# Attention, four experts and a gated MLP on one core: the experts' tail as a ranked list, W2's loads first on GpSimd's queue, GELU without GpSimd, w_out's last row in thirds

## The chip, the cores and the metric

The kernel runs on one core of one Trainium2 chip. A core has TensorE (PE, matmuls), VectorE (DVE), ScalarE (ACT), GpSimd (POOL) and SyncE (SP, which here only issues DMAs). Each engine works its own instruction stream in order and waits on semaphores for the others. The metric is the device time of one execution in microseconds; lower is better.

## The reference

Three layers in a row, in float32, for 4 batches of 448 positions. The inputs are random; cut to what is computed:

```python
# 1: attention, 12 heads of 64, scores capped
scores = cap * np.tanh(scale * (q @ k.T) / cap)
x = softmax(scores) @ v                       # 4 x 448 x 768
# 2: four experts, of which each position takes two
logits = x @ w_gate
topk = np.argpartition(-logits, 2, axis=-1)[..., :2]
w = softmax over the two chosen logits
for e in range(4):
    a = softmax(causal(scale * (x @ wq[e]) @ (x @ wk[e]).T))
    out += chosen(e) * w[e] * (a @ (x @ wv[e]) @ wo[e])
# 3: MLP with spatial gating
h = gelu(x @ w_in)                            # tanh form, 0.044715
u, v = halves of h (512 columns each)
v_s = w_sg @ (layernorm(v) * g_ln) + b_sg     # over positions
return x + (u * v_s) @ w_out
```

## The kernel before

**Numbers.** Where more than single precision's fast form is needed, a matrix is held as two rounded parts, hi and lo (names in _h and _l, type fp32r), and a product is three matmuls; transposes, the experts' scores and the attention run in plain fp32. `rnd` makes the hi part on a chosen engine ("v" VectorE, "a" ScalarE, "p" GpSimd), `rest` the lo part. The weight w_out comes in double precision, and `w_out(k, i, ...)` turns one half of a row k (384 columns) into hi and lo: a load, bit operations on VectorE (tiles `wum`), three operations on GpSimd (tiles `wuw`), and two stores to DRAM (`wud`), from which `wu_h` and `wu_l` are loaded later.

**Stages.** Attention runs in 25 slots, one pair of heads each: six slots make a batch. In the first slots the product W2 = wo w_in is made besides and stored (`w2d`). The experts of a batch follow its attention by some slots; what of them goes into which slot stands in `PLAN`: `queries_keys` (18 matmuls each, tile qk), `values_chunk` (18 matmuls, tile v; its last four columns are the gate's logits, copied to lg), `weigh` (scores `a` of a chunk of 112 positions, a mask operation with the row's maximum on VectorE, exp on ScalarE into `pe`), `gates`, `settle` (reciprocals on VectorE, then eight scalings of pe on GpSimd), `turn` (transposes `tr` of pe, evicted to `pt`), `attend` (16 matmuls av, evicted to y). A batch's attention output is finished by `sums` (matmuls with onehot), `invert` (a copy, an addition, a RECIPROCAL of 128x448 on VectorE, a store rd), broadcast loads `rb` by `load_rb`, the multiplication os by rb in `over_sums`, and the split into xh and xl in `in_parts`; `normed` says in which slot.

**Order.** Up to slot 24 all instructions of TensorE, VectorE, ScalarE and GpSimd are held in program order. Behind it stands the tail: the experts of the last two batches and the whole MLP. There the framework's scheduler chooses, by a timeline of its own and by priorities, which follow the order of the code and `tc.high_priority`. `experts_end` gives the tail's experts slot by slot from the same `PLAN`; `together` weaves them with the parts of the MLP. `mlp_a(b)` makes v (hv, four chunks of six matmuls; GELU, normalization, split into vh and vl), `mlp_b(b)` makes u (hu) and the gate products (sp), `mlp_c(b)` the six output rows (o). `mlp_weights(0)` issues the loads of W2 (`w2_h`, `w2_l`) on GpSimd's queue, and `more_weights` loads wo, and wu_h and wu_l when all eight halves of w_out are done (`wu_done`). The halves 29 to 31 of `W_OUT` fall into the tail. `gelu2` takes its scratch from the six buffers of tag tmp. Matmuls appear at L119, transposes at L461 and all other recorded operations at L104, whichever function issues them.

Of the kernel before, what the change touches and what calls it, by code (L numbers as in the profile page):

```python
# [33 lines left out]
LAG, RATIO, LRATIO, AHEAD, EQ, ORD, L1, EL, WC, NCST, D0, D1, D2, PB, XE, SE, START, WARM, Q2, CK, PE, CP_, AD, WR, KD, PTA, PTE, XHA, LGA, SL, GL, YL, GA, GB = 0.4, .9, .35, 150, 1, 3, 1, 1, 500, 1, 3, 3, 2, 1, 1, 0, 500, 12, 1, 2, 0, 0, 0, 6, 0, 4, 2, 4, 4, 0, 0, 0, 1, 0  # L34
GC = float(np.float32(np.sqrt(2.0 / np.pi)))


def drain(gen):
# [34 lines left out]
def build(ctx: ExitStack, tc: tile.TileContext, a: dict):  # L73
# [179 lines left out]
    def slot(i, side):  # L253

        if i == 0:
            ld[0] = load_pair(*pairs[0])
            ld[1] = load_pair(*pairs[1])
        if i + 2 < len(pairs):  # L260
            qk = [at.tile([128, S], F32, tag=t, name=f"{t}{i + 2}", bufs=3) for t in ("qp", "kp")]
            b, hp = pairs[i + 2]
            nc.sync.dma_start(qk[1], a["kT"][b, :, hp, :])
            nc.sync.dma_start(qk[0], a["qT"][b, :, hp, :])
            ld[i + 2] = qk
        if i < len(pairs):
            first = scores(*pairs[i], 0, *ld[i][:2])
            drain(islice(first, 2))
            side("a")
            drain(first)  # L270
        else:
            side("a")
        side("w")
        if i:
            b, hp = pairs[i - 1]
            drain(values(b, hp, ld.pop(i - 1)[2]))
        if 0 < i < len(pairs) - 1:
            b, hp = pairs[i + 1]
            vv = at.tile([CP, 2, NC, D], F32, tag="vv", name=f"vv{b}_{hp}", bufs=3)
            nc.sync.dma_start(vv, a["v"][b, :, 2 * hp:2 * hp + 2])  # L280
            ld[i + 1] = (*ld[i + 1], vv)
        side("a")
        if i < len(pairs):
            drain(scores(*pairs[i], 1, *ld[i][:2]))
        side("p")
        if i:
            b, hp = pairs[i - 1]
            if hp % 2 == 1:
                drain(sums(b, hp // 2))
        if i < len(pairs):  # L290
            add_up(*pairs[i])
        side("n")
# [16 lines left out]
    def in_parts(b, h2):  # L309

        if h2 == 0:
            X[b] = (xp.tile([128, KC, S], F32R, tag="xh", name=f"xh{b}"),
                    xp.tile([128, KC, S], F32R, tag="xl", name=f"xl{b}"))
        (xh, xl), x, o = X[b], os_t.pop((b, h2)), slice(2 * h2, 2 * h2 + 2)
        rnd("v", xh[:, o, :], x)
        rest("v", xl[:, o, :], x, xh[:, o, :])

    def normed(n, place):

        b = (n - 1) // HP - 1  # L320
        step = (n % HP, place)
        if n > B * HP + 4 or b < 0:
# [20 lines left out]
    wu_done = []  # L343

    def w_out(k, i, pool, *tags):

        o = slice(i * DM // 2, (i + 1) * DM // 2)
        w = pool.tile([128, DM], F32R, tag=tags[0], name=f"wuw{k}_{i}")
        me = pool.tile([128, DM], I32, tag=tags[1], name=f"wum{k}_{i}")
        hi, lo = w[:, :DM // 2], w[:, DM // 2:]  # L350
        nc.sync.dma_start(w.bitcast(I64), a["w_out"][:, k, o])
        yield WC
        p, e = from64(w, me[:, :DM // 2], me[:, DM // 2:])
# [5 lines left out]
        wu_done.append((k, i))  # L359
        yield 1.0  # L360

    def queries_keys(b, ep, t):
        xh, xl = X[b]
# [56 lines left out]
        dve.reciprocal(gs, gs)  # L420
        dve.tensor_tensor(wt, wt, gs.unsqueeze(2).to_broadcast([CP, NC, E]), op=ALU.mult)

    def weigh(b, ep, i):

        qk = QKT[b, ep]
        if i == 0:
            for el in range(2):
                CSS[b, ep, el] = sm.tile([CP, NC], F32, tag=f"cs{el}", name=f"cs{b}_{ep}_{el}")
        n = (i + 1) * CP
        qi = slice(i * CP, (i + 1) * CP)  # L430
        gs = [ps_g.tile([128, 512], F32, tag="g", name=f"a{b}_{ep}_{el}_{i}") for el in range(2)]
        for el in range(2):
            r = slice(64 * el, 64 * el + 64)
            mm(gs[el][:CP, :n], qk[r, 0, qi], qk[r, 1, :n], start=True, stop=True)
        for el, g in enumerate(gs):

            m = sm.tile([CP, 1], F32, tag="m", name=f"m{b}_{ep}_{el}_{i}", bufs=4)
            dve.tensor_tensor_reduce(g[:CP, :n], g[:CP, :n], neg[:, S - n:], -1.0, BIG, ALU.add, ALU.min, m)
            pe = PES[b, ep, el, i] = mo.tile([CP, n], F32, tag=f"pe{i}", name=f"pe{b}_{ep}_{el}_{i}", bufs=4)
            act.activation(pe, g[:CP, :n], AF.Exp, bias=m, scale=-1.0, accum_out=CSS[b, ep, el][:, i:i + 1])  # L440
        yield 1.667 * n + 20.0

    def settle(b, ep):

# [48 lines left out]
    def planned(n):  # L493

        work = {"a": [], "s": [], "w": [], "p": [], "t": [], "n": []}
        for b in reversed(range(B)):
            for place, f, *args in PLAN.get(n - (b + 1) * HP - 4, []):
                work[place].append((b, f, args))
        return work

# [8 lines left out]
    def experts_weights(n, place):  # L509
# [13 lines left out]
        if place == "w" and n in parts:  # L523
# [7 lines left out]
    ws = {n: w_out(*divmod(u, 2), *W_OUT[n][1:]) for u, n in enumerate(W_OUT)}  # L531

    def beside(n):

# [21 lines left out]
                    next(ws[n + 1])  # L556
        return side

    def experts_end(n):

        for m in range(n, B * HP + 20):
            work = planned(m)
            for place in "asw":
                yield from run(work[place])
            for place in ("w", "a1"):
                normed(m, place)
            yield from together(run(work["p"]), run(work["t"]), 0.3)
            yield from run(work["n"])
            normed(m, "n")
            if m in W_OUT:  # L570
                yield from ws[m]


    def prepare_weights(pool):
# [79 lines left out]
        slot(n, beside(n))  # L654
    ah.close()
    pe_pin[0] = False
    ex = experts_end(B * HP + 1)

# [22 lines left out]
    def mlp_weights(part):  # L681
        if part == 1:
            yield from more_weights()
            return
        for k in range(2):
# [11 lines left out]
        yield 1.0  # L697

    def more_weights():
        for k in range(2):  # L700
            for i in range(2):
                o = slice(i * DM // 2, (i + 1) * DM // 2)
                t = tmp(f"wo{k}_{i}")[:, :DM // 2]
                nc.sync.dma_start(t, a["wo"][:, k, o])
                rnd("pav"[int(GB) % 10], wo_h[:, k, o], t)
                rest("pv"[int(GB) // 10], wo_l[:, k, o], t, wo_h[:, k, o])
        while len(wu_done) < 8:
            yield 500.0
        for w, d in ((wu_h, wu_d[0]), (wu_l, wu_d[1])):
            for k in range(0, 4, 2):  # L710
                nc.gpsimd.dma_start(w[:, k:k + 2, :], d[:, k:k + 2, :])
        yield 1.0

    def gelu2(out, h, p, n, nm):

        s = tmp(f"gs{nm}")[:p, :n]
        act.activation(s, h, AF.Square)
        pool_e.tensor_scalar(s, s, 0.044715, 1.0, op0=ALU.mult, op1=ALU.add)
        dve.tensor_tensor(s, s, h, op=ALU.mult)
        act.activation(s, s, AF.Tanh, scale=GC)  # L720
        dve.scalar_tensor_tensor(out, s, 1.0, h, op0=ALU.add, op1=ALU.mult)

# [115 lines left out]
        drain(together(mlp_c(2), mlp_b(3), 13440 / C))  # L838
        drain(mlp_c(3))
    elif ORD == 3:  # L840
        drain(together(ex, mlp(((mlp_a, 0), (mlp_b, 0), (mlp_weights, 1), (mlp_a, 1), (mlp_c, 0), (mlp_b, 1), (mlp_a, 2))), LRATIO))
# [69 lines left out]
```

## Time and profile before

| | before |
|---|---|
| median of 3 runs | 559.38 us (558.11 to 561.81) |
| profiled execution | 559.72 us, of which the span on the core is 558.0 |
| TensorE busy | 532.7 us, 95% |
| VectorE busy | 361.4 us, 65% |
| ScalarE busy | 325.7 us, 58% |
| GpSimd busy | 141.4 us, 25% |
| chain that ended last | PE 73%, DVE 16%, ACT 6%, DMA 2% |

The shares are means over the span. Attention fills the first 283 us or so and the tail the rest; VectorE and ScalarE are nearly idle in the last 80 us, and nearly full in parts of the stretch from 290 to 350. The page gives TensorE's clock in tenths of full speed: full speed is 2.4 GHz, and the lower level is 1.2.

### The profile page before, as it was taken

How to read it: one execution, taken by the hardware profiler on the slowest of the kernel's cores; microseconds unless marked ns; L12 is line 12 of the kernel's file. 1: busy time of each engine (PE TensorE's matmuls, PEld its weight loads, DVE VectorE, ACT ScalarE, POOL GpSimd, SP SyncE). 2: the span in 40 equal slices, each digit the busy share in tenths (PEclk: the TensorE clock that was granted, in tenths of full speed). 3: DMA queues.
4: the chain of work that ended last, by engine and by line, in shares of the span. 5: the costliest groups of instructions: out<-in, count | busy, mean ns of one | idle time of the engine just before them, and what ended most of it. 6: DMA issues, size and time to landing. Idle time of an engine off the chain costs nothing.

```text
span 558.0 us, 7562 instructions
## 1 busy us (share of the span) xinstructions
PE 532.7 (95%) x2732; PEld 346.3 (62%) x2732; DVE 361.4 (65%) x725; ACT 325.7 (58%) x508; POOL 141.4 (25%) x180
## 2 busy tenths in 40 slices
PE   7999999899999989999988989999999989999997
PEld 2333333455555554656557655878768879889996
DVE  3899999984666636567567599676631786485300
ACT  5988888688687896577822345353534344253211
POOL 0000122141155251243340364515521131031000
PEclk9999999999999999999999978999999999999999
DMA  8974615752424141322056221010421000000111
GB/s 246 338 217 123 207 51 160 223 175 80 130 67 142 50 140 49 103 71 67 22 158 165 54 59 58 29 58 0 162 101 64 2 0 34 33 34 33 51 49 66
DMA packets 30596, 53.97 MB, mean 97 GB/s; under 512 B 3872, under 2 KB 22880, under 8 KB 30560
## 3 DMA queue, kind: packets, MB, share of 16 engines
q1 hardware_dynamic: 29408, 48.26, 28.2%
q0 software_dynamic: 1152, 5.24, 2.8%
q8 instruction: 21, 0.34, 0.3%
q14 instruction: 15, 0.12, 0.1%
HBM read 41.83 MB, written 11.67 MB: 96 GB/s over the span
## 4 chain that ended last, share of the span: by engine, by line
PE 73%; DVE 16%; ACT 6%; DMA 2%; issue 2%; POOL 1%; DVEq 0%; POOLq 0%; ACTq 0%; SPq 0%
PE o L119 15%; PE po L119 10%; PE s L119 10%; PE qk L119 8%; PE sp L119 7%; PE v L119 5%; ACT p L104 4%; PE a L119 3%; PE hv L119 3%; PE hu L119 3%; PE w2ps L119 2%; PE tr L461 2%; PE av L119 2%; DVE pb L104 2%; DVE rs L104 2%
## 5 line engine op out<-in xcount | busy, mean ns | idle before, releaser
L104 ACT ACTIVATE p<-s,tsc 112x896 f32<-112x896 f32 x96 | 91.4, 1005 | 24.4 <-PE s L119 24.4
L119 PE MATMUL s<-qp,kp 64*112 64x448 f32 x384 | 84.4, 557 | 3.4 <-ACT p L104 3.4
L104 ACT ACTIVATE p<-p,capt 112x1792 f32<-112x1792 f32 x48 | 85.9, 1790 | 1.3
L104 POOL TENSOR_TENSOR pb<-p 112x896 f32<-112x896 f32 x18 | 38.9, 2163 | 166.6 <-ACT p L104 96.9
L119 PE MATMUL po<-p,vv 112*64 112x448 f32 x384 | 77.3, 545 | 0.0
L104 DVE TENSOR_TENSOR pb<-pb,p 112x896 f32<-112x896 f32 x48 | 57.3, 1194 | 16.0 <-ACT p L104 12.3
L119 PEld LDWEIGHTS s<-qp,kp 64*112 64x112 f32 x384 | 30.8, 172 | 50.6 <-issue 21.3
L119 PEld LDWEIGHTS po<-p,vv 112*64 112x64 f32 x384 | 25.5, 136 | 45.0 <-issue 44.0
L104 ACT ACTIVATE pe<-a,m 112x112 f32<-112x112 f32 (+3 forms) x64 | 31.2, 491 | 25.3 <-DVE m L104 24.5
L104 POOL TENSOR_SCALAR pe<-pe,cs 112x112 f32<-112x112 f32 (+1 forms) x64 | 31.6, 519 | 50.3 <-DVE cs L104 50.2
L104 DVE CUSTOM_DVE_ANT_0 a<-a,neg 112x112 f32<-112x112 f32 (+3 forms) x64 | 27.7, 464 | 20.0 <-PE a L119 20.0
L119 PE MATMUL qk<-xh,wqk_h 128*128 128x448 f32 x96 | 38.2, 398 | 2.6 <-DVE xh L104 2.6
L119 PE MATMUL o<-gh,wu_h 128*128 128x448 f32 x96 | 35.6, 371 | 0.8 <-DMA wu_h<-wud 0.8
L119 PE MATMUL o<-gl,wu_h 128*128 128x448 f32 x96 | 35.6, 371 | 0.0
L119 PE MATMUL qk<-xh,wqk_l 128*128 128x448 f32 x96 | 35.4, 369 | 0.0
L119 PE MATMUL a<-qk 64*112 64x112 f32 (+3 forms) x128 | 29.9, 440 | 5.6 <-ACT pe L104 3.4
L119 PE MATMUL o<-gh,wu_l 128*128 128x448 f32 x96 | 35.0, 370 | 0.0
L104 ACT ACTIVATE ob<-o 128x448 f32<-128x448 f32 x24 | 13.0, 541 | 31.5 <-PE o L119 31.3
L119 PE MATMUL v<-wvg_h,xh 128*112 128x260 f32 x96 | 28.7, 299 | 0.7 <-ACT pe L104 0.7
L461 PE MATMUL tr<-ident,pe 112*112 112x112 f32 x160 | 23.7, 261 | 4.9 <-DVE lg L104 1.8
L119 PE MATMUL v<-wvg_h,xl 128*112 128x260 f32 x96 | 27.1, 283 | 0.0
L119 PE MATMUL v<-wvg_l,xh 128*112 128x260 f32 x96 | 27.1, 282 | 0.0
(226 smaller groups left out, 1096.5 us busy)
## 6 DMA issues: line engine op xcount, KB each, us to landing
kp<-in_kT_dram SPq DMA_DIRECT2D x24, 224.0 KB, 3.1
qp<-in_qT_dram SPq DMA_DIRECT2D x24, 224.0 KB, 3.2
vv<-in_v_dram SPq DMA_DIRECT2D x24, 224.0 KB, 3.1
rb<-rd SPq DMA_DIRECT2D x24, 224.0 KB, 4.7
out_dram<-ob SPq DMA_DIRECT2D x24, 224.0 KB, 1.9
wuw<-in_w_out_dram SPq DMA_DIRECT2D x8, 384.0 KB, 3.5
wud<-wuw SPq DMA_DIRECT2D x16, 192.0 KB, 1.9
ws<-in_wqk_dram SPq DMA_DIRECT2D x4, 384.0 KB, 6.0
```

The lines of the kernel that those rows point to most:

```text
L104: ins = f(*args, **kw)
L119: pin(nc.tensor.matmul(*args, **kw))
L461: pin(nc.tensor.transpose(g[:CP, j * CP:(j + 1) * CP], pe[:, j * CP:(j + 1) * CP], ident))
```

## The change

Seven things change, all of them around the tail.

- `experts_end` no longer reads `PLAN`: the tail's experts are one list, `steps()`, and each step is given out at a high priority, ahead of all of the MLP.
- In slot 24 `sums` and `invert` of the last batch come ahead of the experts' work of that slot instead of behind it.
- `weigh` may take two chunks, whose scores share a PSUM bank.
- W2's loads have the highest priority on their queue (12000 instead of 4000).
- `gelu2` does without GpSimd: the square is scaled by the root of 0.044715 on ScalarE, and VectorE adds 1 and multiplies in one operation.
- The first half of w_out's row 2 stays in slot 23; its second half now falls into slot 24, and row 3 is done in three parts of 256 columns within the MLP's list, in tiles of tag tmp (two to a part). `more_weights` waits for the last projections (`projected`) instead of `wu_done`.
- `PTA` goes from 4 to 3, so that the evictions of turn (1,1) go from VectorE to ScalarE, and the last batch's xh is rounded on ScalarE instead of VectorE.

```diff
-LAG, ... KD, PTA, PTE, ... = ..., 0, 4, 2, ...
+LAG, ... KD, PTA, PTE, ... = ..., 0, 3, 2, ...
+GQ = float(np.float32(np.sqrt(0.044715)))
...
+        if i == len(pairs):
+            drain(sums(B - 1, HP // 2 - 1))
+            invert(B - 1)
         side("p")
-        if i:
+        if 0 < i < len(pairs):
...
-        rnd("v", xh[:, o, :], x)
+        rnd("a" if b == B - 1 else "v", xh[:, o, :], x)
...
-    def weigh(b, ep, i):
+    def weigh(b, ep, *chunks):
...
     W_OUT = {11: ("w", xp, "rb0", "rb1"), 14: ("n", at, "ws", "ws"), 17: ("w", at, "ws", "ws"),
-             20: ("n", at, "ws", "ws"), 23: ("w", at, "ws", "ws"),
-             29: ("n", xp, "rb0", "rb1"), 30: ("n", xp, "rb0", "rb1"), 31: ("n", xp, "rb0", "rb1")}
+             20: ("n", at, "ws", "ws"), 23: ("w", at, "ws", "ws"), 24: ("n", at, "ws", "ws")}
...
+        def steps():
+            yield from weigh(b, 0, 2)
+            yield from turn(b - 1, 1, 1)
+            yield from values_chunk(b, 2)
+            yield from weigh(b, 0, 3)
+            yield from values_chunk(b, 3)
+            gates(b)
+            settle(b, 0)
+            yield from queries_keys(b, 1, 0)
+            yield from attend(b - 1, 1)
+            yield from queries_keys(b, 1, 1)
+            yield from turn(b, 0, 0)
+            over_sums(l, 0)
+            over_sums(l, 1)
+            load_rb(l, 2)
+            yield from weigh(b, 1, 0, 1)
...
+        todo = steps()
+        while True:
+            with tc.high_priority(4000):
+                cost = next(todo, None)
...
+        if part == 2:
+            for i in range(3):
+                yield from w_out(3, i, 3, *[lambda dt, name: ml.tile([128, 512], dt, tag="tmp", name=name, bufs=6)] * 2)
+            return
         for k in range(2):
-            with tc.high_priority(4000):
+            with tc.high_priority(12000):
                 nc.gpsimd.dma_start(w2_h[:, k, :], w2_d[0][:, k, :])
...
     def more_weights():
+        while not projected:
+            yield 500.0
...
-        act.activation(s, h, AF.Square)
-        pool_e.tensor_scalar(s, s, 0.044715, 1.0, op0=ALU.mult, op1=ALU.add)
-        dve.tensor_tensor(s, s, h, op=ALU.mult)
+        act.activation(s, h, AF.Square, scale=GQ)
+        dve.scalar_tensor_tensor(s, s, 1.0, h, op0=ALU.add, op1=ALU.mult)
...
-        drain(together(ex, mlp(((mlp_a, 0), (mlp_b, 0), (mlp_weights, 1), (mlp_a, 1), ...
+        drain(together(ex, mlp(((mlp_a, 0), (mlp_weights, 2), (mlp_b, 0), (mlp_weights, 1), (mlp_a, 1), ...
```

How the instructions stand shows three places best. The first is VectorE at the end of slot 24. In the kernel before, the last batch's sums (rs) and the first split of the MLP's y (yh, yl) come there among the masks (ISA) of batch 2:

```order
L104 TENSOR_TENSOR rs_2017<-rs_2017,sum_2_2432 128x448
L104 CAST yh_2503<-y_1431 128x896
L104 ISA a_0_0_2_2491,m_0_0_2_2495<-a_0_0_2_2491,neg 112x336
L104 ISA m_0_0_2_2495 112x1
L104 RECIPROCAL rs_2017<-rs_2017 128x448
L104 TENSOR_TENSOR yl_2504<-y_1431,yh_2503 128x896
L104 ISA a_0_1_2_2492,m_0_1_2_2499<-a_0_1_2_2492,neg 112x336
```

In the changed kernel rs and its RECIPROCAL come just ahead of these rows, which hold the copies lg of batch 2's values chunks 1 and 2, the bit operations (wum) of w_out's half (2,1) and two of the three multiplications os by rb:

```order
L105 COPY lg_2388<-v_1_2410 112x4
L105 TENSOR_SCALAR wum_1_2320<-wuw_1_2319 128x384
L105 ISA a_0_1_2_2515,m_0_1_2_2522<-a_0_1_2_2515,neg 112x336
L105 ISA m_0_1_2_2522 112x1
L105 TENSOR_SCALAR wum_1_2320<-wum_1_2320 128x384 x2
L105 TENSOR_TENSOR os_0_1790<-os_0_1790,rb_0_2381 128x896
L105 SCALAR_TENSOR_TENSOR wum_1_2320<-wuw_1_2319,wum_1_2320 128x384
L105 TENSOR_TENSOR os_2_2062<-os_2_2062,rb_1_2384 128x896
L105 TENSOR_SCALAR wum_1_2320<-wum_1_2320 128x384
L105 SCALAR_TENSOR_TENSOR wum_1_2320<-wuw_1_2319,wum_1_2320 128x384
L105 COPY lg_2388<-v_2_2558 112x4
```

The reciprocal moved ahead of two masks, and os, which stood behind all masks of this pair, moved ahead of the copy lg of chunk 2.

The second place is GpSimd's queue behind the settling of batch 1's second pair (pe). In the kernel before:

```order
L104 TENSOR_SCALAR pe_1_1_3_2285<-pe_1_1_3_2285,cs_1_1_2127 112x448
L687 DMA w_h<-w2d_81 128x1024 x2
L688 DMA w_l<-w2d_82 128x1024 x2
L104 TENSOR_SCALAR gsv_0_2567<-gsv_0_2567 112x512
L104 TENSOR_SCALAR gsv_1_2659<-gsv_1_2659 112x512
```

In the changed kernel:

```order
L105 TENSOR_SCALAR pe_1_1_3_2285<-pe_1_1_3_2285,cs_1_1_2127 112x448
L105 TENSOR_SCALAR wuw_1_2319<-wum_1_2320 128x384
L105 TENSOR_TENSOR wum_1_2320<-wum_1_2320,wuw_1_2319 128x384
L105 TENSOR_TENSOR wuw_1_2319<-wum_1_2320 128x384
L751 DMA w_h<-w2d_81 128x1024 x2
L752 DMA w_l<-w2d_82 128x1024 x2
L105 TENSOR_SCALAR pe_0_0_0_2330<-pe_0_0_0_2330,cs_0_0_2322 112x112
```

W2's loads moved behind the three operations on w_out's half (2,1), which is held in program order, and GELU's operations (gsv) are gone.

The third place is TensorE at the gate products (sp) of batch 2 and output row 1 (o) of batch 1. In the kernel before, the products of the second chunk of positions and then the output row:

```order
L119 MATMUL sp_0_4068<-sg_h,vh_3924 128x448
L119 MATMUL sp_0_4068<-sg_l,vh_3924 128x448
L119 MATMUL sp_0_4068<-sg_h,vl_3925 128x448
L119 MATMUL o_1_4092<-yh_3422,wo_h 128x448
L119 MATMUL o_1_4092<-yl_3423,wo_h 128x448
L119 MATMUL o_1_4092<-yh_3422,wo_l 128x448
```

In the changed kernel, from the last product of the first chunk on:

```order
L120 MATMUL sp_0_4054<-sg_h,vl_3917 128x448
L120 MATMUL o_1_4078<-yh_3525,wo_h 128x448
L120 MATMUL o_1_4078<-yl_3526,wo_h 128x448
L120 MATMUL o_1_4078<-yh_3525,wo_l 128x448
L120 MATMUL sp_0_4054<-sg_h,vh_3916 128x448
L120 MATMUL sp_0_4054<-sg_l,vh_3916 128x448
```

Three of the output row's matmuls moved between the two chunks, and the second chunk's product with vl moved behind the other fifteen.

## Rows read from the trace of the kernel before

**Rows 1.** The page: TensorE's share; its granted clock in 40 slices, in tenths.

```profile
PE 532.7 (95%) x2732; PEld 346.3 (62%) x2732; DVE 361.4 (65%) x725; ACT 325.7 (58%) x508; POOL 141.4 (25%) x180
...
PEclk9999999999999999999999978999999999999999
```

**Rows 2.** What TensorE waited for from 285 us: total, times, longest.

```profile
PE a L119 <- ACT pe L104: 3.4, 3, 2.2
PE a L119 <- ACT qk L104: 1.3, 1, 1.3
PE tr L461 <- ACT pt L104: 0.9, 2, 0.4
PE o L119 <- DMA wu_h<-wud: 0.8, 1, 0.8
...
PE tr L461 <- POOL pe L104: 0.7, 1, 0.7
```

**Rows 3.** Busy time by stage: engines, then PEclk, DMA share, GB/s.

```profile
290.00:300.00 10.00, 7.82 (x45) 4.60 (x38) 8.37 (x20) 2.94 (x9) 1.07 (x2) 1.00 0.60 192
...
340.00:350.00 10.00, 8.73 (x23) 5.42 (x22) 9.33 (x29) 6.83 (x16) 2.82 (x5) 0.66 0.14 41
...
450.00:460.00 10.00, 8.53 (x38) 6.97 (x37) 9.38 (x21) 4.56 (x8) 3.46 (x6) 0.97 0.00 0
460.00:470.00 10.00, 10.00 (x44) 9.14 (x44) 7.83 (x15) 5.26 (x10) 1.69 (x3) 0.86 0.06 23
```

**Rows 4.** VectorE's timeline from 287 us: start, duration, operation, [idle before].

```profile
292.06 2.94 DVE L104 RECIPROCAL rs<-rs 128x448 f32<-128x448 f32 x1
...
302.40 1.09 DVE L104 TENSOR_TENSOR os<-os,rb 128x896 f32<-128x896 f32 x1 [2.06 <-DMA rb<-rd]
...
304.26 1.10 DVE L104 TENSOR_TENSOR os<-os,rb 128x896 f32<-128x896 f32 x1 [0.18 <-DMA rb<-rd]
```

**Rows 5.** TensorE's timeline, 309 to 329 us.

```profile
309.17 2.10 PE L119 MATMUL av<-pt,vp 112*64 112x448 f32 x14
311.20 0.47 PE L119 MATMUL qk<-xh,wqk_h 128*128 128x448 f32 x1
311.51 0.36 PE L119 MATMUL qk<-xh,wqk_l 128*128 128x448 f32 x1
...
328.91 4.00 PE L119 MATMUL av<-pt,vp 112*64 112x448 f32 x16
```

**Rows 6.** GpSimd's timeline at 286 us.

```profile
286.05 1.29 POOL L687 DMA_DIRECT2D w_h<-w2d  x2
```

**Rows 7.** Instructions on the tile wuw: ns min/median/max, first and last start.

```profile
L104 POOL TENSOR_SCALAR wuw<-wum x8: 508/524/1279, 120.7 to 352.4; 128x384 fp32r<-128x384 f32 x8
L104 POOL TENSOR_TENSOR wum<-wum,wuw x8: 1004/1020/1727, 121.3 to 354.7; 128x384 f32<-128x384 f32 x8
...
DMA to landing us min/median/max: 1.8/1.9/4.4
```

**Rows 8.** DMA issues from 280 to 420 us: KB each, us to landing.

```profile
wu_l<-wud POOLq DMA_DIRECT2D x2, 768.0 KB, 9.1
...
w_h<-w2d POOLq DMA_DIRECT2D x2, 512.0 KB, 4.7
```

**Rows 9.** Timelines of TensorE and of VectorE, 455 to 500 us.

```profile
457.14 0.48 PE L119 MATMUL sp<-sg_h,vh 112*128 112x448 f32 x1 [0.72 <-ACT vh L104]
...
458.33 0.47 PE L119 MATMUL sp<-sg_h,vl 112*128 112x448 f32 x1 [0.51 <-DVE vl L104]
...
455.48 0.95 DVE L104 TENSOR_SCALAR vg<-vg,mv,rstd 112x512 f32<-112x512 f32 x1
...
499.77 0.55 DVE L104 TENSOR_SCALAR vg<-vg,mv,rstd 112x512 f32<-112x512 f32 x1
```

**Rows 10.** VectorE's timeline at the gates of the last batch.

```profile
384.93 1.10 DVE L104 TENSOR_TENSOR gt<-gt,eq 112x64 f32<-112x64 f32 x1
```

**Rows 11.** Instructions on the tile gsv (GELU of v).

```profile
L104 POOL TENSOR_SCALAR gsv<-gsv x16: 619/622/1102, 304.7 to 496.2; 112x512 f32<-112x512 f32 x16
```

More of the change, by code (lines that the diff above doesn't have):

```diff
@@ L341, in normed, with w_out @@
             in_parts(b, 2)
[L343 to L350, printed above, removed]
+    projected = []
+    def w_out(k, i, of, w, me):
+        n = DM // of
+        o = slice(i * n, (i + 1) * n)
+        w, me = w(F32R, f"wuw{k}_{i}")[:, :2 * n], me(I32, f"wum{k}_{i}")[:, :2 * n]
+        hi, lo = w[:, :n], w[:, n:]
         nc.sync.dma_start(w.bitcast(I64), a["w_out"][:, k, o])
         yield WC
-        p, e = from64(w, me[:, :DM // 2], me[:, DM // 2:])
+        p, e = from64(w, me[:, :n], me[:, n:])
         rnd("p", hi, p)
@@ L358, in w_out, with scratch @@
             nc.sync.dma_start(wu_d[t][:, k, o], (hi, lo)[t].bitcast(F32))
-        wu_done.append((k, i))
         yield 1.0
+    def scratch(pool, *tags):
+        return [lambda dt, name, tag=tag: pool.tile([128, DM], dt, tag=tag, name=name) for tag in tags]
     def queries_keys(b, ep, t):
@@ L421, in gates @@
         dve.tensor_tensor(wt, wt, gs.unsqueeze(2).to_broadcast([CP, NC, E]), op=ALU.mult)
[L423 removed]
+    def weigh(b, ep, *chunks):
         qk = QKT[b, ep]
[L426 removed]
+        if 0 in chunks:
             for el in range(2):
                 CSS[b, ep, el] = sm.tile([CP, NC], F32, tag=f"cs{el}", name=f"cs{b}_{ep}_{el}")
[L429 to L435, printed above, removed]
+        gs = [ps_g.tile([128, 512], F32, tag="g", name=f"a{b}_{ep}_{el}_{chunks[0]}") for el in range(2)]
+        parts, o = [], 0
+        for i in chunks:
+            n = (i + 1) * CP
+            for el, g in enumerate(gs):
+                r = slice(64 * el, 64 * el + 64)
+                mm(g[:CP, o:o + n], qk[r, 0, i * CP:n], qk[r, 1, :n], start=True, stop=True)
+                parts.append((i, el, n, g[:CP, o:o + n]))
+            o += n
+        for i, el, n, g in parts:
             m = sm.tile([CP, 1], F32, tag="m", name=f"m{b}_{ep}_{el}_{i}", bufs=4)
[L438 removed]
+            dve.tensor_tensor_reduce(g, g, neg[:, S - n:], -1.0, BIG, ALU.add, ALU.min, m)
             pe = PES[b, ep, el, i] = mo.tile([CP, n], F32, tag=f"pe{i}", name=f"pe{b}_{ep}_{el}_{i}", bufs=4)
[L440 to L441 removed]
+            act.activation(pe, g, AF.Exp, bias=m, scale=-1.0, accum_out=CSS[b, ep, el][:, i:i + 1])
+        yield 1.667 * o + 20.0
     def settle(b, ep):
@@ L496, in planned @@
         for b in reversed(range(B)):
-            for place, f, *args in PLAN.get(n - (b + 1) * HP - 4, []):
+            step = n - (b + 1) * HP - 4
+            for place, f, *args in PLAN.get(step, []):
                 work[place].append((b, f, args))
@@ L557, in beside, with experts_end @@
         return side
[L559 to L571, printed above, removed]
+    def experts_end():
+        b, l = B - 2, B - 1
+        def steps():
[14 more added lines that the diff above has]
+            yield from weigh(b, 1, 0, 1)
+            yield from turn(b, 0, 1)
+            in_parts(l, 0)
+            yield from weigh(b, 1, 2)
+            yield from attend(b, 0)
+            in_parts(l, 1)
+            yield from weigh(b, 1, 3)
+            settle(b, 1)
+            over_sums(l, 2)
+            in_parts(l, 2)
+            yield from queries_keys(l, 0, 0)
+            yield from turn(b, 1, 0)
+            yield from queries_keys(l, 0, 1)
+            yield from weigh(l, 0, 0, 1)
+            yield from turn(b, 1, 1)
+            yield from values_chunk(l, 0)
+            yield from weigh(l, 0, 2)
+            yield from attend(b, 1)
+            yield from values_chunk(l, 1)
+            yield from weigh(l, 0, 3)
+            yield from values_chunk(l, 2)
+            yield from values_chunk(l, 3)
+            gates(l)
+            settle(l, 0)
+            yield from queries_keys(l, 1, 0)
+            yield from queries_keys(l, 1, 1)
+            projected.append(l)
+            yield from weigh(l, 1, 0, 1)
+            yield from turn(l, 0, 0)
+            yield from weigh(l, 1, 2)
+            yield from turn(l, 0, 1)
+            yield from weigh(l, 1, 3)
+            yield from attend(l, 0)
+            settle(l, 1)
+            yield from turn(l, 1, 0)
+            yield from turn(l, 1, 1)
+            yield from attend(l, 1)
+        todo = steps()
+        while True:
+            with tc.high_priority(4000):
+                cost = next(todo, None)
+            if cost is None:
+                return
+            yield cost
```

13 lines of the change are left out of this document (6 added, 7 removed).

## The prediction

> **What bounds the kernel now.** I read the engines' shares first: TensorE is busy 532.7 of 558.0 us, and its granted clock dips in the 24th and 25th of 40 slices, 321 to 349 us [rows 1]. So matmul work sets the time, and the change, which removes no matmul, can win or lose only in TensorE's idle time and in the time at the lower clock. Up to about 283.5 us (the last slots of attention) both programs stand alike, instruction for instruction, so I read what follows: TensorE's own waits from 285 us on [rows 2], the granted clock by stage [rows 3], then the stages that hold the losses. The waits add up to some 11 us, in pieces of 0.3 to 2.2. A mean clock of 0.66 over ten microseconds (340 to 350) means that 3.4 of them were lost at 1.2 GHz, behind an idle 1.27 us for a qk eviction [rows 2, 3]. Earlier the clock fell after an idle 2.23 us: the 16 av matmuls there took 4.00 us, where 14 took 2.10 at 2.4 GHz [rows 5]; that is 1.6 lost, and with the rows around it I put it at 2.3. A third dip, around 460 us, costs 0.3 and 1.4 in two windows, 1.7 [rows 3]. After 283.5 us the kernel thus loses about 7.4 us to the clock and 11 to idling. **I price each fall of the clock at 3.4 us**, by the one window that holds a whole one.
>
> The sum is made against the profiled execution's own 559.72 us (span 558.0); the median of the runs is 559.38, 0.06% less.
>
> **The change part by part.**
>
> *Sums and inversion of the last batch ahead of the experts' work.* In the kernel before, the RECIPROCAL of 2.94 us stands at 292.06, ahead of yl and of masks that TensorE waits for [rows 4]. TensorE is busy 7.82 of the ten us from 290 [rows 3]; the 2.18 that lack are three waits behind that RECIPROCAL (a for pe, hu for yl, v for pe), and they go. After the change the sums' matmuls stand where the values of batch 2 begin, at 283.5; with the same 1.0 us until VectorE adds them, 0.6 for that and 2.94, the reciprocal is done at about 288.05 instead of 295.0. The first two os multiplies start 7.4 and 9.3 us behind its end [rows 4], because the broadcast loads are awaited; so they would start at 295.45 and 297.3, and the second one is done at 298.4. But both now stand, with bit operations of w_out's half between them, ahead of the copy lg out of values chunk 2 (the order of VectorE, above), and TensorE's chunk 3 needs that copy. Counting matmuls from 283.5 at the durations of the trace, TensorE comes to chunk 3 at 297.4 and may start it at 299.5: **2.15 us of new idling**. The evictions of turn (1,1), all eight on ScalarE now, I put at 1.25 us between 287 and 297: at least nothing, at most three of some 0.6 each. Net +1.2.
>
> *W2's loads.* They were issued from 286.05 on [rows 6]. Now they stand behind the three GpSimd operations of w_out's half (2,1) (the order of GpSimd, above), 0.52, 1.02 and 1.02 us [rows 7], which wait for the bit operations behind the second os: issue near 302. Landing takes 4.7 us by the row of w_h and 9.1 by the slowest row of that queue [rows 8]: 307 to 311. The first hv now stands behind both key projections, at about 311, so I take nothing, since qk and av hide it; with 9.1, and w_l behind w_h, it is up to 3 us.
>
> *From 311 to 348.* Gone are the waits tr for pe 0.68, tr for pt 0.44, a for pe 2.23 and a for qk 1.27 [rows 2], 4.6 us, and the dips of 2.3 and 3.4: 10.3. In their place: VectorE was about full there, 9.33 of 10 us from 340 on [rows 3], and keeps its work, since the new GELU has two VectorE operations as the old one had. It sheds only the rounding of xh, three operations of about 1 us, which go to ScalarE (6.83 of 10 [rows 3]). So I expect late masks and evictions again: 0.3 and 0.4 early on, and for vh and vl of the first batch between 0.7 (the wait for vh at 457 [rows 9]) and 2.2 (the longest wait of before [rows 2]); I take 1.5, the middle. The thirds are new there. Their six tiles come from the pool that GELU draws on, and GpSimd works them off behind the eight settling operations: two thirds of 2.56 us [rows 7] is 1.7, three of them 5.1, and then a store of 1.9 us [rows 7]. The last tile comes free 7 us after the settling, when the fourth hu wants one: 1.6 us by counting on, bounds 0 and 1.6. That is 3.8 us of new idling, in pieces like those behind which the clock fell; I take **one fall, 3.4**. Net 3.8 + 3.4 - 10.3 = -3.1.
>
> *wu's loads* no longer wait for the last halves' stores but for the projections; between the last qk and their first use there are now some 7.9 us of other matmuls, where before there were 4.3. The 0.8 us for wu_h [rows 2] goes: -0.8.
>
> *Around the last gates.* Beside GpSimd's rounding of wo a small gate operation of 112x64 takes 1.10 us [rows 10]. In the new order transposes of batch 3's first pair wait for what VectorE and ScalarE have queued behind the gates: 0 to 2.5 us; I take the middle, 1.25.
>
> *The tail around 457.* TensorE waits 0.72 for vh, 0.51 for vl [rows 9] and 0.24 for what follows, 1.47, and the clock falls (1.7). The chain behind it runs through GELU on GpSimd, 0.62 us an operation, 16 of them for v alone [rows 11], and these operations are awaited. Without that link each chunk's chain is shorter by 0.62 and a hand-over; a normalization took 0.95 beside GpSimd and 0.55 without it [rows 9]; and output row 1's matmuls now stand ahead of the last vl products of the first pair of chunks (the order of TensorE, above). I take all of it, -3.2; were the chain as late as before, nothing.
>
> On that last point the Trainium skill (SBUF — State Buffer, "Who interferes with whom") has a rule: VectorE in a two-port mode, tensor_scalar among them, and GpSimd lock each other out of a shared port pair for the whole instruction. The rows of 0.95 and 0.55 agree. By the rule alone every GpSimd operation that goes would give its length back on VectorE, which would take the 1.5 and the 1.25 above to nothing, and 2.75 us off the sum.
>
> *Switches.* The order of TensorE changes between fp32 and the rounded kind six times more often; the first qk behind an av takes 0.47 where the next takes 0.36 [rows 5]: six times 0.11, +0.7.
>
> Sum: 1.2 - 3.1 - 0.8 + 1.25 - 3.2 + 0.7 = -3.95, and 559.72 - 3.95 = **555.8 us**.
>
> **The rivals.** (a) *No fall of the clock* in the new stalls: 2.18 us of idling in pieces between 290 and 300 left the clock at 1.00 [rows 3], so pieces below a microsecond may pass. 555.8 - 3.4 = 552.4; with 0.7 for vh and vl, nothing for the thirds and nothing at the gates it is 3.65 less, and with the evictions of turn (1,1) in time another 1.25: down to 547.5. (b) *Two falls*, the second at the gates or at 299: 559.2, no change. (c) *W2 late*: the loads land past 311 and hv waits up to 3 us in one piece, with a fall: 555.8 + 6.4 = 562.2. The 9.1 us speak for it; against it, wu's loads were larger and went out together [rows 8]. The Trainium skill (SBUF — State Buffer, "SBUF: two separate sides") has the rule that loads issued from GpSimd's queue starve of descriptors while VectorE runs two-port operations; by it (c) would be the likely case. In the trace w_h landed in 4.7 us while VectorE was busy 8.37 of 10, which speaks against it [rows 3, 8]. (d) *Slower: each of the four new stalls* (299, near 341, 347, the gates) brings a fall, which is so if idle pieces of 1.3 us and up suffice, as at 341 in the trace: 552.4 + 4 x 3.4 = 566.0. Against it: after a stall the engines that were late have caught up, so the next one shrinks. (e) *The list does nothing*: VectorE is as full as before, the losses move, and the time stays at 559.7.
>
> **How the numbers follow.** Forecast 0.34; (a) 0.30; (b) and (e) together 0.19; (c) 0.10; (d) 0.07. A measurement of this kernel tells about 1% from no change, 5.6 us: faster is below 553.8, slower above 565.0. The values taken from the middle of their bounds can move the forecast by 2 us and more; a third of its chance lies below 553.8, and with (a) faster is 0.42. Slower is (d) and the ends of (b) and (c) with longer stalls, 0.12. The rest, 0.46, is within 1%. The range runs from 547.5, the low end of (a), to 562.2, case (c); (d) is left out.
>
> **What would show it.** Right: the sums' matmuls at 283.5 and the first os near 295.4; chunk 3's v behind a wait for lg of about 2 us; w_h issued near 302 and no wait of hv for it; the wait for wu_h gone; no dip of the clock around 460, and one between 297 and 350. Wrong: hv waiting for w_h or w_l; three dips or more; waits for vh and vl at 457 as long as before; hu waiting several microseconds for a tile that a third holds.

## The result, and the profile after

The changed kernel takes 552.5 us (median of 12 runs, 551.18 to 557.11) where the kernel before took 558.95 in the same session; the ratio is 0.990, with a 95% interval of 0.9875 to 0.9921. The forecast was 555.8, the range 547.5 to 562.2. Six of the twelve times lie at 551.2 to 551.9 with a mean granted clock of 0.996 or 0.997, five at 556.1 to 557.1 with 0.983 to 0.987, and the profiled execution, 553.08 (span 551.0), lies between at 0.993; a hundredth of the clock is 5.5 us of this span.

The page of the changed kernel, TensorE's shares and its clock in 40 slices. One slice is dimmed where before two were [rows 1], and the busy time is 5.1 us shorter though no matmul went, because fewer of them ran at 1.2 GHz:

```profile
PE 527.6 (96%) x2732; PEld 344.1 (62%) x2732; DVE 351.7 (64%) x720; ACT 331.0 (60%) x519; POOL 128.9 (23%) x151
...
PEclk9999999999999999999999999999899999999999
```

What TensorE waited for from 283 us on (total, times, longest). Every wait of [rows 2] is gone but the one for pt; three new ones hold most of the 8.3 us that are left of the 10.3 that the same view lists before:

```profile
PE hu L120 <- DVE u L105: 2.6, 1, 2.6
PE tr L470 <- ACT pe L105: 2.1, 1, 2.1
PE v L120 <- DVE lg L105: 1.8, 1, 1.8
PE tr L470 <- ACT pt L105: 1.3, 3, 0.5
PE v L120 <- ACT pe L105: 0.3, 1, 0.3
PE a L120 <- ACT pt L105: 0.2, 1, 0.2
```

Busy time by stage, columns as in [rows 3]. The clock stays at 1.00 from 290 to 390 us, through the longest idle piece of all (340 to 350), falls once behind the wait of the transposes, and does not fall at 450:

```profile
340.00:350.00 10.00, 7.27 (x41) 6.09 (x39) 4.64 (x12) 3.52 (x8) 9.84 (x15) 1.00 0.21 67
...
390.00:400.00 10.00, 7.94 (x38) 6.14 (x37) 6.98 (x22) 4.90 (x15) 4.96 (x9) 0.83 0.77 269
...
450.00:460.00 10.00, 10.00 (x51) 9.26 (x50) 8.00 (x18) 5.56 (x10) 1.41 (x2) 1.00 0.06 23
```

VectorE's timeline in the changed kernel, which answers to [rows 4]. The reciprocal ends at 290.2 instead of 295.0, the first os starts 7.2 us behind its end, the second 9.1, and the copy lg comes behind both:

```profile
287.28 2.95 DVE L105 RECIPROCAL rs<-rs 128x448 f32<-128x448 f32 x1
...
297.45 1.09 DVE L105 TENSOR_TENSOR os<-os,rb 128x896 f32<-128x896 f32 x1 [1.68 <-DMA rb<-rd]
...
299.36 1.09 DVE L105 TENSOR_TENSOR os<-os,rb 128x896 f32<-128x896 f32 x1 [0.35 <-DMA rb<-rd]
...
301.23 0.15 DVE L105 COPY lg<-v 112x4 f32<-112x4 f32 x1
```

These times stand 2.1 us too late for a comparison with [rows 4]: the sums' matmuls came at 285.60 instead of the 283.5 of the forecast, because the attention ahead of them, the same instructions in both kernels, took longer in this execution (a score matmul at 8.92 instead of 8.11 us, and a mean clock of 0.96 instead of 1.00 from 80 to 120). That is not the change's doing: the two profiled runs below that put the new GELU into the kernel before have the same dip (0.83 from 110 to 120). So behind the sums the profiled gain is 7.0 + 2.1 = 9.1 us. It is mostly busy time, 260.06 us of TensorE before and 252.85 now, and to 1.9 us idle time; before, then after, columns as in [rows 3]:

```profile
283.52:558.00 274.48, 260.06 (x1314) 214.10 (x1312) 157.32 (x354) 104.03 (x238) 72.45 (x115) 0.97 0.18 58
```

```profile
285.60:551.00 265.40, 252.85 (x1314) 210.58 (x1312) 147.52 (x349) 109.35 (x249) 59.88 (x86) 0.99 0.20 62
```

GpSimd's timeline in the changed kernel. W2's loads (to [rows 6]) are issued at 304.1, and the eight settling operations at 337 take 7.57 us, with the thirds' nine operations behind them:

```profile
304.13 1.29 POOL L751 DMA_DIRECT2D w_h<-w2d  x2
...
336.97 7.57 POOL L105 TENSOR_SCALAR pe<-pe,cs 112x112 f32<-112x112 f32 x8
...
346.63 1.43 POOL L105 TENSOR_TENSOR wuw<-wum 128x256 fp32r<-128x256 f32 x2
```

### The profile page after: what moved, and what is told of

It is laid out like the page before. It is cut to its first block, busy times and chain, and to the rows that moved or that the text cites. A ratio compares the mean times of both kernels' runs of the same rounds, so it can differ in the third digit from the quotient of the medians.

```text
span 551.0 us, 7552 instructions
## 1 busy us (share of the span) xinstructions
PE 527.6 (96%) x2732; PEld 344.1 (62%) x2732; DVE 351.7 (64%) x720; ACT 331.0 (60%) x519; POOL 128.9 (23%) x151
## 4 chain that ended last, share of the span: by engine, by line
PE 77%; DVE 10%; ACT 5%; DMA 3%; POOL 2%; issue 2%; SPq 1%; POOLq 0%; DVEq 0%; ACTq 0%
PE o L120 15%; PE po L120 10%; PE s L120 10%; PE qk L120 8%; PE sp L120 6%; PE v L120 5%; PE hv L120 4%; PE a L120 4%; PE hu L120 4%; ACT p L105 4%; PE av L120 3%; PE w2ps L120 2%; PE tr L470 2%; DMA rb<-rd 2%; DVE rs L105 2%
## 5 line engine op out<-in xcount | busy, mean ns | idle before, releaser
L105 POOL TENSOR_SCALAR pe<-pe,cs 112x112 f32<-112x112 f32 (+1 forms) x64 | 39.7, 643 | 55.7 <-DVE cs L105 53.9
L105 POOL TENSOR_TENSOR rstd<-rstd,mhalf 112x1 f32<-112x1 f32 x16 | 10.2, 639 | 100.9 <-DVE rstd L105 100.9
L470 PE MATMUL tr<-ident,pe 112*112 112x112 f32 x160 | 25.2, 263 | 6.4 <-ACT pe L105 2.1
L120 PE MATMUL a<-qk 64*112 64x112 f32 (+3 forms) x128 | 27.9, 427 | 1.0 <-ACT qk L105 0.9
L105 ACT ACTIVATE pt<-tr 112x112 f32<-112x112 f32 (+3 forms) x40 | 15.7, 404 | 19.4 <-PE tr L470 19.0
```

Of the source, the lines that this page charges most:

```text
L105: ins = f(*args, **kw)
L120: pin(nc.tensor.matmul(*args, **kw))
L470: pin(nc.tensor.transpose(g[:CP, j * CP:(j + 1) * CP], pe[:, j * CP:(j + 1) * CP], ident))
```

## The experiments

The theory to begin with, A: the gain is the sum of named waits and of the dips behind them, and each part of the change owns some. The rival, B, that the list alone carries it; and O, which the first four runs brought up: the tail's order comes out of a scheduler, and what an edit costs is mostly the order that the scheduler then makes. In "free order" the scheduler chooses the tail's order, as in both kernels; with "order held" it is written down. Times are medians, ratios are to the kernel before, run on the same chip, whose own median lay between 558.95 and 559.89 us in these groups of runs.

| run | time us | ratio (95%) |
|---|---|---|
| changed kernel | 552.5 | 0.990 (0.9875 to 0.9921) |
| old GELU, free order | 565.35 | 1.010 (1.006 to 1.014) |
| before with the new GELU, free order | 562.07 | 1.0055 (1.002 to 1.009) |
| late sums, free order | 564.12 | 1.009 (1.006 to 1.011) |
| halves in place of thirds, free order | 560.86 | 1.003 (1.000 to 1.0055) |
| old GELU in the changed kernel's order | 566.19 | 1.011 (1.008 to 1.014) |
| new GELU in the order of before | 556.74 | 0.996 (0.994 to 0.998) |
| lg first, order held | 554.14 | 0.990 (0.987 to 0.994) |
| three moves, order held | 548.04 | 0.9805 (0.978 to 0.983) |
| thirds first, order held | 549.37 | 0.983 (0.980 to 0.986) |
| four moves, order held | 546.1 | 0.9765 (0.974 to 0.979) |
| lg on ScalarE, free order | 561.11 | 1.0035 (1.002 to 1.0055) |
| list at ordinary priority, free order | 552.74 | 0.988 (0.985 to 0.990) |

**One part undone, the order left to the scheduler.** First the GELU, in the changed kernel:

```diff
-        act.activation(s, h, AF.Square, scale=GQ)
-        dve.scalar_tensor_tensor(s, s, 1.0, h, op0=ALU.add, op1=ALU.mult)
+        act.activation(s, h, AF.Square)
+        pool_e.tensor_scalar(s, s, 0.044715, 1.0, op0=ALU.mult, op1=ALU.add)
+        dve.tensor_tensor(s, s, h, op=ALU.mult)
```

> The changed kernel with the old GELU (GpSimd's operation in the chain), all else kept. Theory A (the chain through GpSimd made TensorE wait around 457 us and the clock fall): waits of sp for vh and vl of 0.5 us or more come back near 450, with a dip of the clock there, and the time rises by 1.5 to 4.9 us, to 554 to 557.5. Theory B (the list carries the gain, GELU is hidden beside it): within 1 us of the changed kernel, about 552.5.

565.35 us, more than either theory gave. The waits that A named came back near 460 (0.7 us for vh, 0.5 behind it), but without a dip: the clock is 1.00 from 440 to 480. TensorE's timeline of this run has two larger waits that neither named, both of the experts' transposes; the second is let go by a GELU operation on GpSimd:

```profile
351.61 0.78 PE L470 MATMUL tr<-ident,pe 112*112 112x112 f32 x3 [3.58 <-ACT pt L105]
...
396.93 0.38 PE L470 MATMUL tr<-ident,pe 112*112 112x112 f32 x2 [3.46 <-POOL gsv L105]
```

The same edit the other way, the new GELU alone in the kernel before (the diff above with its signs exchanged):

> The kernel before with the new GELU alone. Theory A: the waits for vh and vl around 457 us and the dip behind them go, 3.2 us, and VectorE is freer from 310 to 350: about 554.5. Theory B (the list carries the gain): no change, 558 to 560.

562.07, slower than the kernel before by 0.55%: both theories missed. The waits at 457 us are gone, as A has it, but the waits for pe stay and those for pt grow from 0.9 to 2.9 us; the waits of this run:

```profile
PE a L120 <- ACT pe L105: 3.3, 3, 2.2
PE tr L462 <- ACT pt L105: 2.9, 4, 1.2
```

The last batch's sums and inversion back behind the experts' work of slot 24:

```diff
-        if i == len(pairs):
-            drain(sums(B - 1, HP // 2 - 1))
-            invert(B - 1)
         side("p")
-        if 0 < i < len(pairs):
+        if 0 < i:
             b, hp = pairs[i - 1]
             if hp % 2 == 1:
                 drain(sums(b, hp // 2))
+            if i == len(pairs):
+                invert(B - 1)
```

> The changed kernel with the last batch's sums and inversion back behind the experts' work of slot 24. Theory A (the early inversion only trades one stall for another): the wait of v for lg of 1.8 us goes, waits for masks and yl behind the reciprocal of about 2 us come back, time within 1 us of 552.5. Theory C (the early inversion matters because os, and with it the last batch's projections, come 7 us earlier): stalls of some microseconds ahead of the last batch's first qk, 555 or more.

564.12: the number of theory C (a late inversion costs), at another place than it named. VectorE and then TensorE in this run: the third os waits 7.68 us for its load, and the split yh of the MLP's input, queued behind it on VectorE, is what hv waits 6.00 us for. So the late inversion costs where the scheduler lines something up behind os; the transposes' waits for the settling, 4.9 us in all, and a mean clock of 0.74 from 320 to 340 stand beside it:

```profile
314.36 1.09 DVE L105 TENSOR_TENSOR os<-os,rb 128x896 f32<-128x896 f32 x1 [7.68 <-DMA rb<-rd]
315.37 0.16 DVE L105 TENSOR_REDUCE gs<-wt 112x4 f32<-112x16 f32 x1
315.44 0.62 DVE L105 CAST yh<-y 128x896 fp32r<-128x896 f32 x1
```

```profile
316.12 2.05 PE L120 MATMUL hv<-w_h,yh 128*112 128x512 f32 x4 [6.00 <-DVE yh L105]
```

Row 3 of w_out in two halves in the buffers rb0 and rb1 instead of three thirds in GELU's:

```diff
-            for i in range(3):
-                yield from w_out(3, i, 3, *[lambda dt, name: ml.tile([128, 512], dt, tag="tmp", name=name, bufs=6)] * 2)
+            for i in range(2):
+                yield from w_out(3, i, 2, *scratch(xp, "rb0", "rb1"))
```

> The changed kernel with w_out's row 3 in two halves in the buffers rb0 and rb1, within the MLP's list as the thirds were, so that no part of w_out holds a tile of GELU. Theory A (the thirds hold GELU's tiles): the wait of hu for u of 2.6 us goes, and the time falls by about 2.6, to 550. Rival: the work on w_out just moves, a wait of like size appears elsewhere (for wu_h, or for rb), 552.5 or more.

560.86. hu's wait is gone, as expected, and the rival came true beyond its size; TensorE's waits of this run are for W2, whose loads now stand behind more work on GpSimd and are issued at 307, and for xh:

```profile
315.70 1.16 PE L120 MATMUL hv<-w_h,yh 128*112 128x512 f32 x4 [2.31 <-DMA w_h<-w2d]
...
319.25 0.48 PE L120 MATMUL hv<-w_l,yh 128*112 128x512 f32 x1 [1.68 <-DMA w_l<-w2d]
...
339.82 0.74 PE L120 MATMUL qk<-xh,wqk_h 128*128 128x448 f32 x1 [3.39 <-ACT xh L105]
```

Four edits, four times 8 to 13 us against the changed kernel or 3 against the one before, with most of the waits at places that the edits do not touch: that suggests theory O. To test a part by itself, the order has to be held.

**The order held.** The order in which each engine's instructions came out was written into the kernel as a table and imposed by edges that carry no semaphore. No run times the table without an edit, but the trace of the run that moves one copy (lg first) has every recorded operation of TensorE, VectorE, ScalarE and GpSimd in the changed kernel's order except that copy:

```diff
+    for eng, (skip, order) in ORDER.items():
+        made = [i for i in nc.cur_bb.bb.instructions
+                if str(i.engine).split(".")[1] == eng and str(i.opcode) != "TilePoolBoundary" and i.name not in loose]
+        for p, q in zip([skip - 1] + order, order):
+            tc.add_manual_dep(made[q], made[p].name,
+                              mybir.DependencyInfo(mybir.DependencyClass.NoSync, mybir.DependencyReason.DATA),
+                              reason="order")
```

First both GELUs again, with the first diff and its opposite. In the changed kernel's order, only GpSimd's 32 operations are put where the scheduler likes:

> The changed kernel with every engine's order held as it is, by a table, and only the GELU put back to the form with GpSimd (its 32 operations go where GpSimd's scheduler puts them). Theory A (what an undone part costs lies mostly in the order that the scheduler then makes, little in the part itself): the longer GELU chain brings back some waits of 0.3 to 0.7 us for vh and vl, the time rises by 0 to 5 us, 552 to 557, far from the 565 of the freely ordered kernel with the same GELU. Theory B (the GELU itself is worth it): about 562 to 565 again.

566.19: this run's theory B, that the GELU itself is worth it, and against O. Here the old GELU costs 13.7 us with not one matmul in another place, as much as in free order. TensorE's waits from 283 us on add up to 14.7 us instead of 8.3, and the clock falls three times behind 300 us instead of once (0.83 from 300 to 310, 0.68 and 0.81 from 350 to 370, 0.66 from 400 to 410). The timelines of GpSimd, VectorE and TensorE in this run show the longest wait: one GELU operation of 0.62 us stands behind the rounding of wo and the settling on GpSimd, VectorE waits 4.84 us for it, and TensorE 3.82 for a buffer that the chain behind it holds:

```profile
389.66 3.93 POOL L164 TENSOR_TENSOR wo_l<-wo,wo_h 128x384 fp32r<-128x384 f32 x4
395.32 3.83 POOL L164 TENSOR_SCALAR pe<-pe,cs 112x112 f32<-112x112 f32 x8 [1.73 <-DVE cs L164]
...
399.75 0.62 POOL L164 TENSOR_SCALAR gsv<-gsv 112x512 f32<-112x512 f32 x1
```

```profile
400.41 0.69 DVE L164 TENSOR_TENSOR gsv<-gsv,hv 112x512 f32<-112x512 f32 x1 [4.84 <-POOL gsv L164]
```

```profile
402.53 0.74 PE L179 MATMUL o<-yh,wo_h 128*128 128x448 f32 x1 [3.82 <-DVE vg L164]
```

Whether another place for these operations on GpSimd would cost less was not tried. In the order of before:

> The kernel before with every engine's order held as it is and only the GELU without GpSimd. Theory A: the waits for vh 0.72 and vl 0.51 around 457 us shrink or go, the dip of the clock behind them with them, VectorE's operations beside GpSimd get shorter: 1 to 4 us less, 555.5 to 558.5, where the freely ordered kernel with the same GELU took 562. Theory B (GELU was hidden): 559.4, no change.

556.74, 2.3 us less, theory A. Of the waits of [rows 9] the one for vh is gone, and no dip follows the 0.5 that stays in vl's chain; the other waits of [rows 2] stand, but the one for qk is 0.4 instead of 1.3, and the dip that followed it, the largest of before, is gone as well. Two others came, in the attention (0.83 from 110 to 120) and at 0.83 from 400 to 410. The windows of this run:

```profile
340.00:350.00 10.00, 9.61 (x41) 7.04 (x40) 9.34 (x29) 6.34 (x15) 1.30 (x2) 1.00 0.20 61
...
450.00:460.00 10.00, 9.19 (x43) 7.56 (x43) 9.39 (x24) 5.21 (x10) 1.64 (x3) 1.00 0.00 0
460.00:470.00 10.00, 10.00 (x51) 9.25 (x50) 8.03 (x16) 5.20 (x10) 0.55 (x1) 1.00 0.13 48
```

With the run of the same GELU in free order this separates the two: the part is worth -2.3 us in the order of before, over the whole kernel and not at 457 us alone, and the order that the scheduler made of it +5.3.

**Single waits, in the changed kernel's held order.** One entry of VectorE's table moved, the copy lg of chunk 2 ahead of the second os:

> The changed kernel with its order held, and one instruction moved: VectorE's copy lg of chunk 2 ahead of the second os multiplication. If the wait of v for lg, 1.8 us, is what the second os costs: it shrinks to 0.3 or less, and the time falls by 1 to 1.8 us, to 551; more if a dip of the clock went with it. If the work behind is late anyway (the rounding of xh waits for os): the time stays at 552.5 and another wait takes its place.

The median, 554.14, says little, since four of the six runs had a lower clock (0.987 to 0.994); the two at 0.996 took 550.18 and 551.92, where the changed kernel at that clock took 551.2 to 551.9. TensorE's waits of this run show why so little: the 1.8 for lg went, and 0.9 for pe and 0.5 for w_l came, so 0.4 was left. The second of the two outcomes expected, nearly:

```profile
PE hu L179 <- DVE u L164: 2.6, 1, 2.6
PE tr L529 <- ACT pe L164: 2.1, 1, 2.1
PE tr L529 <- ACT pt L164: 1.3, 3, 0.5
PE qk L179 <- ACT pe L164: 0.9, 1, 0.9
PE hv L179 <- DMA w_l<-w2d: 0.5, 1, 0.5
```

Only the thirds' nine operations moved on GpSimd, ahead of the last four of the settling:

> The changed kernel with its order held and only the thirds' nine GpSimd operations moved, ahead of the second half of the settling of batch 2's second pair. If hu's wait of 2.6 us for u is worth its length: it goes, the waits of 1.8 for lg and 2.1 for pe stay, 549 to 550.5. If the time is set behind it by something else: 552 to 553, with a new wait between 345 and 395 us.

549.37, as if the wait were worth its length: it is gone, five of six runs are at 0.996 or 0.997 with 548.4 to 549.8 (2.4 us under the changed kernel at that clock), and the wait of the transposes shrank as well, to 1.5. GpSimd in this run: the first four settling operations still take 5.25 us, the last four, with VectorE done with wum and at work on gsu, u and vs, 1.93:

```profile
337.07 5.25 POOL L164 TENSOR_SCALAR pe<-pe,cs 112x112 f32<-112x112 f32 x4
...
348.57 1.93 POOL L164 TENSOR_SCALAR pe<-pe,cs 112x112 f32<-112x112 f32 x4
```

Both moves, and a third, the masks and exps of batch 3's second pair ahead of the MLP's normalization on VectorE and ScalarE:

> As the run with lg first, and two more moves in the held order: on GpSimd the nine operations of the thirds between the two halves of the settling of batch 2's second pair, and on VectorE and ScalarE the first four masks and exps of batch 3's second pair ahead of the MLP's normalization. If each wait is worth its length: hu's wait of 2.6 us for u goes, the transposes' wait of 2.1 for pe falls under 0.5 and no dip follows it: 5 to 8 us less than the changed kernel, 544.5 to 547.5. If the stalls only move down the line: 550 to 552.5.

548.04, between the two outcomes, 4.5 us under the changed kernel. All three waits went, and the mean clocks are 0.993 to 1.000. New are waits for loads that the earlier TensorE runs into:

```profile
PE o L179 <- DMA wu_h<-wud: 1.3, 1, 1.3
PE o L179 <- DMA wu_l<-wud: 1.1, 1, 1.1
...
PE hv L179 <- DMA w_l<-w2d: 0.8, 1, 0.8
```

A fourth move, GpSimd's issue of wu's loads:

> The three moves, and a fourth: GpSimd issues wu_h's loads ahead of the last settling of batch 3's first pair and wu_l's in its middle, instead of both behind it. If the waits for wu_h 1.3 and wu_l 1.2 us of the run with three moves are the issue's place on the queue: both go, 545 to 546.5. If the loads cannot start sooner (their buffers come free with the last qk) or the settling is late by as much: 547.5 to 549.

546.1: both waits went, as the first outcome has it. The loads now start as soon as the last projection frees their buffers (GpSimd issues wu_h's at 382.02, behind a wait of 0.50 for qk), and 1.4 us for w_l is the longest wait left. This version beats both kernels, by 2.35% and 1.2%.

**How far the order is chance.** Two more edits of the changed kernel in free order. Batch 2's four copies lg, 112x4 each, on ScalarE:

```diff
-        dve.tensor_copy(LG[b][:, c, :], g[:CP, E * HD:E * HD + E])
+        if b == B - 2:
+            act.activation(LG[b][:, c, :], g[:CP, E * HD:E * HD + E], AF.Copy)
+        else:
+            dve.tensor_copy(LG[b][:, c, :], g[:CP, E * HD:E * HD + E])
```

> The changed kernel, freely ordered by the scheduler, with one small thing changed: batch 2's four copies lg (112x4) on ScalarE. By the copies alone the wait of v for lg of 1.8 us would go, 550.5 to 552.5, as with lg moved in the held order. If the changed kernel's time hangs on the one order that the scheduler happened on, and any small change makes it fall upon another: 556 to 565, with waits at places that have nothing to do with lg.

561.11, 8.6 us for an edit of four small copies, 0.17 us each on ScalarE. The wait for lg is gone; the largest in its place is one of av for an exp of another stage. That exp's mask stands on VectorE behind the third os, which waits 7.97 us for its load, as in the run with the late sums (7.68); in the changed kernel that os waits 1.64. So two of the free orders lose most at one place. TensorE, then VectorE:

```profile
310.36 2.87 PE L120 MATMUL av<-pt,vp 112*64 112x448 f32 x6 [5.74 <-ACT pe L105]
```

```profile
307.85 1.09 DVE L105 TENSOR_TENSOR os<-os,rb 128x896 f32<-128x896 f32 x1 [7.97 <-DMA rb<-rd]
308.86 0.62 DVE L105 CUSTOM_DVE_ANT_0 a<-a,neg 112x448 f32<-112x448 f32 x1
```

And the list without its priority:

```diff
-            with tc.high_priority(4000):
-                cost = next(todo, None)
+            cost = next(todo, None)
```

> The changed kernel, freely ordered, with the tail's list of experts at the ordinary priority instead of ahead of the MLP. If the ranking carries the gain: 558 or more, with the waits of the kernel before between 310 and 350. If not, and the order stays good: 551 to 554.

552.74: the ranking carries nothing that the time shows. The order differs in places (hu's wait for u is 0.5, v's for lg 1.9, and others are new), and the time is the same. W2's higher priority was not tested by a run.

## Why the prediction was right, and where not

The time fell inside the range, on the side of rival (a), 552.4, which had 0.30. That the median stands on (a)'s number is partly luck: behind the sums the gain is 9.1 us and not (a)'s 7.3, 2.1 us were lost ahead of the change, and one fall of the clock did come, at the gates. The order, read against the trace of before, gave the new waits at their places; two sizes and the clock were off. Term by term, in the profiled executions:

- *Sums ahead*, +1.2: measured +0.5. The wait of v for lg is 1.80 (forecast 2.15), the small waits for evictions 1.14 (1.25), against 2.18 and 0.30 that went. The steps stood: first os 7.2 us behind the reciprocal's end, lg behind both. Taking the wait away brought back only 0.4, since pe and w_l are next; what the early inversion is worth in free order (11.6 us with it undone) belongs to that order.
- *W2's loads*, nothing: no wait, but without the slack that was claimed. They were issued at 304.13 and landed in 6.9 us (w_h) and 9.9 (w_l), not 4.7; w_l's came to some 315.3 and its first matmul stands at 315.54. All four now go out together, 2.1 MB, beside w_sgT's 0.8 MB and two stores, with the DMA engines 0.82 busy from 310 to 320; before they went in two pairs, at 286.05 [rows 6] and 290.77. Rival (c)'s wait shows in the three held orders in which lg moved and TensorE comes earlier: 0.5, 0.8 and 1.4 us. The Trainium skill's rule on starved descriptors (SBUF — State Buffer, "SBUF: two separate sides") is not needed for it: from 304 to 316 the engines moved 3.1 MB, a mean of 259 GB/s, so the bytes fill that time, though no run here excludes a share of it.
- *311 to 348*, -3.1: measured -7.0, **the step that failed**. The waits that it has going (4.6) and the dips (5.7) went, and the thirds wait, 1.6 at most, came as 2.60. But the wait for vh and vl, taken as 1.5, did not come (VectorE was busy 27.7 of 38 us from 311 on where before it was 31.5; with the old GELU in this order it does not come there either, so the GELU is not the reason), and **no fall of the clock** came, 3.4. The price itself was one of two sizes: the one fall of this trace cost 1.7, like the dip at 460 of before. The bound of 1.6 for the thirds was too low; the settling ahead of them took 7.57 us, where those of the kernel before take 3.84 to 4.68 (the prediction names no length), and with the thirds ahead of its second half the wait was gone.
- *wu's loads*, -0.8: gone. *The tail*, -3.2: no wait and no dip between 440 and 470. The run with the new GELU in the old order gives 2.3 for the GELU alone, the shorter wait and the lost dip near 341 included.
- *Around the gates*, +1.25: the transposes wait 2.06, within the bounds, and the one fall of the clock is here, 1.7 more. Before's 0.4 and 0.4 near 375, which the sum left out, went.

Together +0.5 - 7.0 - 0.8 - 3.2 + 3.8 - 0.8 = -7.5 of the 9.1; the switches, +0.7, do not show as such, so some 1.6 to 2.3 us are not in any named term. They lie in TensorE's busy time, not in a wait: idle time fell by 1.9 us, as the waits in this sum do, and busy time by 7.2, where the dips in it make 5.7. Some 0.3 of that is the first dip of before, whose sixteen av matmuls lost 1.9 us and not 1.6, since sixteen take 2.11 us at 382.02 in the same trace; where the rest lies stays open.

Of the rivals, (b) and (d) did not come: behind the sums the clock fell once, and not behind the stalls at 299 and 347. (e), "the list does nothing", is right as to the ranking (552.74 without it) and wrong as to the time. Two rows say less than the prediction takes from them. Against the starved descriptors it sets w_h's 4.7 us beside VectorE's 8.37 of 10 from 290 on, but w_h, issued at 286.05, had mostly landed by then; w_l, issued at 290.77 (4.4 us), was the load in that window, and a RECIPROCAL filled most of VectorE's time beside it. And the normalization of 0.55 us at 499.77 was not without GpSimd: a gsu operation began at 499.92 and took 0.82 us, where others take 0.57.

What the runs leave open: how much of the gain belongs to the early inversion and to the thirds by themselves. Undone, they make another order, and the order held needs them.

## What to carry to other kernels

Where a scheduler sets the order, undoing one part measures the order that comes out of it: in the kernel before the same GELU was +0.55% in free order and -0.4% in a held one, and four copies of 112x4 cost 1.6%. It need not: the old GELU cost the changed kernel 13 to 14 us in either. Hold the order by a table, move single rows, and read the waits; then a wait of TensorE was worth 0.4 to 2.4 us of its 1.8 to 2.6, whatever came next being the rest, and four moves, read from two traces, gave about as much again as the change. An operation of 0.6 us costs what it is queued behind: on an engine that works in order, look at the long work ahead of it, not at its length.

## What was not expected of the hardware

The eight settling operations on GpSimd took 3.84 us at 284.35, beside masks and a RECIPROCAL on VectorE, and 7.57 at 336.97, beside its bit operations on wum, many of them of the tensor_scalar kind; with the thirds first the last four took 1.93, beside work on gsu, u and vs. The eight at 310.83 took 7.69 beside the splits yl and xl, so wum is not needed for it; no run separates the operations. The Trainium skill (SBUF — State Buffer, "Who interferes with whom") names tensor_scalar among the VectorE operations that can take a port pair shared with GpSimd, the other engine then waiting for the whole instruction; 7.57 against 3.84 agrees with that. The prediction looked only at what GpSimd does to VectorE.

The clock: an idle piece of 2.60 us at 347 left it at 1.00, one of 2.06 at 394 was followed by 1.2 GHz, and runs of one program differ by a hundredth in its mean, 5 us. With the waits gone the spread goes too, as far as four runs show it: those of the four moves lie between 545.9 and 547.2.
